# Sink columns as one float32r product for both heads, weights' first loads at other steps, and another start

## The chip, the cores and the metric

The kernel runs on one core of one Trainium2 chip. The metric is device time in microseconds (us), the median of three runs. The engines are TensorE (PE, with its weight loads as PEld), VectorE (DVE), ScalarE (ACT), GpSimd (POOL) and SyncE (SP), which issues most of the DMAs.

## What is computed

Causal attention with a window of 128 keys and 4 "sink" keys that every query sees, then two feed-forward layers. Batch 2, 8 heads, 768 positions, head size 64; the layers have 512 inputs, 2048 hidden units and 512 outputs, over 1536 tokens.

```python
scores = scale * np.matmul(q, k.transpose(0, 1, 3, 2))
is_sink = pos[None, :] < int(n_sink)
in_window = (rel >= 0) & (rel < int(window))
scores = np.where(is_sink | in_window, scores, -1000000000.0)
a = np.exp(scores - np.max(scores, axis=-1, keepdims=True))
a = a / (np.sum(a, axis=-1, keepdims=True) + 1e-09)
x = np.matmul(a, v)               # heads joined: 1536 x 512
h = x @ w_in;  g = np.where(h >= 1, h, np.where(h <= -1, 0, (h + 1) ** 2 / 4));  x = g @ w_out
h = x @ w2_in; g = h * np.clip(h + 3, 0, 6) / 6;                                 out = g @ w2_out
```

## The kernel before

The attention comes first and takes about a sixth of the time. Its work is cut into 16 pairs: a pair is two heads and up to four blocks of 128 queries (`GROUPS` gives four sorts of pairs, four of each: blocks 0 to 3 of the first batch, blocks 4 and 5, blocks 0 and 1 of the second batch, blocks 2 to 5). A block of a pair is a unit. The host has put the sink keys beside each block's window, so that a unit's scores are one product of up to 260 columns for each head (128 keys of the block before, 4 sinks, 128 keys of its own).

The code makes a list of steps and then runs it; two units are scored, then two units that were scored four units ago are turned, and when a pair is complete it is mixed:

- `load` and `load_v` issue a pair's q, k and v on SP (the first k on ACT). Three buffers of each are there, so a later load waits for an earlier pair's last use. SP works its queue in order.
- `score` (L425): two float32 products on PE; DVE adds the mask and takes the row's extreme (L448); ACT takes the exponentials and their sums (L484).
- `normalise` (L458): DVE makes the reciprocals of the sums (L459, L460); the probabilities are scaled, most of them on POOL (L475), some on ACT or DVE (L477, L479). For units with a separate sink part (w over 256) DVE writes the scaled sink columns into `psk` (L462).
- `turn` (L506): PE transposes the probabilities (L520, L521), ACT or DVE copies them out of PSUM (L502, L504).
- `sinks` (L524): PE transposes a whole pair's `psk` at once (L527), and DVE multiplies it by a mask of ones, `own`, into `pts` (L530), so that each query block keeps only its own 32 rows.
- `mix` (L536): the products with v, for each head its own half of the output partitions (L562). The last two are the sinks' share: `pts` against `vs`, in which v's four sink rows stand for each head in each 32 rows.

`vs` is filled by `load_sinks` (L404): 16 small DMAs on SP straight from v, after a memset on POOL. POOL's first work is a list in order: masks, the identity, then the memsets of `vs`, `own` and `psk` (L582 to L587).

A product with float32r operands is used for the layers: each operand is split into a rounded float32r part and the rest, and three products are added. In the attention all products are float32. PE's and SP's instructions stand in program order; the other engines' order is set by a scheduler at build time, and the names of engines for many copies by a small table of costs.

While the attention runs its last steps, the first weights are loaded in halves (`halves`, L991: the number is of steps left), narrowed from 64 to 32 bits in pieces on ACT and DVE (`narrow`, L184), and the first hidden groups (`h_group`) are put between the steps. Behind the attention the memory of its tiles is used again: `combine_x` (L754) starts with DMAs on POOL's queue (L784), and behind them on that queue stands the spill of a weight tile (L272) whose buffer the next weight waits for.

Of the kernel before, what the change touches and what calls it, by code (L numbers as in the profile page):

```python
# [8 lines left out]
F32 = mybir.dt.float32  # L9
# [7 lines left out]
P = 128  # L17
# [55 lines left out]
def sink_attention_moe_moe_kernel(  # L73
# [257 lines left out]
    NS = sink_columns(n_sink) if fast else 0  # L331
    KB = P + NS
# [13 lines left out]
    def build_fast_attention(at_p):  # L346
# [33 lines left out]
        def load(j):  # L380
# [8 lines left out]
            parts = [slice(0, P), slice(P, 2 * P), slice(2 * P, None)] if j == 0 else [slice(None)]  # L389
# [9 lines left out]
        vs = at_p.tile([P, B, DM], F32, name="vs", bufs=1)  # L399
        pts = [at_p.tile([P, NQ, P], F32, name=f"pts{n}", bufs=1) for n in range(2)]  # L400
        psk = [at_p.tile([P, NQ, SR], F32, name=f"psk{n}", bufs=1) for n in range(DIST)]
        own = at_p.tile([P, NQ], F32, name="own", bufs=1)

        def load_sinks():  # L404
            for b in range(B):
                for e in range(2):
                    for r in range(e * NS, P, SR):
# [17 lines left out]
        def score(j, u):  # L425
# [32 lines left out]
            def normalise():  # L458
                nc.vector.tensor_scalar_add(out=sm, in0=sm, scalar1=1e-9)  # L459
                nc.vector.reciprocal(out=sm, in_=sm)  # L460
                if w > 2 * P:
                    nc.vector.tensor_tensor(  # L462
                        out=psk[j % DIST][:, u - 1:u + 1, 0:2 * NS].rearrange("p u (e s) -> p u e s", e=2),
                        in0=p4[:, :, P:KB].rearrange("p (u e) s -> p u e s", e=2),
                        in1=sm.rearrange("p (u e) -> p u e", e=2).unsqueeze(3).to_broadcast([P, 2, 2, NS]), op=ALU.mult,
                    )
                end = units.index((j, u)) >= len(units) - 4
# [56 lines left out]
        def sinks(j, us, nq):  # L524

            ps = bank("ps_k")[:, 0:P]
            nc.tensor.transpose(ps, psk[j % DIST].rearrange("p u s -> p (u s)"), ident)  # L527
# [8 lines left out]
        def mix(j):  # L536
# [9 lines left out]
            for e in range(2):  # L546
                cs = slice(e * D, (e + 1) * D)
                te = t[:, e].rearrange("p n k q -> p (n k q)")
                for kb in range(nb):
# [4 lines left out]
                    ops[e].append((u0, u1 + 1, tv[:, kb, cs], te[:, c0:c1]))  # L554
                o = 0 if i0 == 0 else 1
                ops[e] = ops[e][o::2] + ops[e][1 - o::2]
                if sink:
                    ops[e].append((us, nq, ts[:, cs], tsink[:, us:nq, :].rearrange("p n q -> p (n q)")))
            for n in range(len(ops[0])):
                for e in range(2):  # L560
                    u0, u1, l, r = ops[e][n]
                    nc.tensor.matmul(  # L562
                        ps[e * D:(e + 1) * D, u0 * P:u1 * P], l, r, start=n == 0, stop=n == len(ops[0]) - 1
                    )
# [10 lines left out]
        def begin():  # L575
            load(0)
            load_v(0)
# [3 lines left out]
            with tc.manual_schedule(engines={mybir.EngineType.Pool}):  # L581
                prepare()  # L582
                make_identity(nc, ident)
                for t in (vs, own, *psk):
                    nc.gpsimd.memset(t, 0.0)
# [397 lines left out]
    with tc.manual_schedule(engines={mybir.EngineType.PE, mybir.EngineType.SP}):  # L983
# [3 lines left out]
        if fast:  # L987
            with tc.tile_pool(name="at", bufs=2) as at_p:
                build_fast_attention(at_p)
                fills = {9: (0, 0, 0), 5: (0, 0, 1), 2: (0, 1, 0)}  # L990
                halves = {56: ("i", 0), 50: ("i", 1), 44: ("o", 0), 36: ("o", 1)}  # L991
# [125 lines left out]
```

## Time and profile before

| | |
|---|---|
| median of 3 runs | 604.55 us (604.28 to 604.63) |
| the profiled execution | 603.75 us, of which 602.0 us are the span from the first to the last instruction |
| PE busy | 590.9 us, 98% |
| DVE busy | 472.3 us, 78% |
| ACT busy | 393.8 us, 65% |
| POOL busy | 109.5 us, 18% |
| chain that ended last | PE 84%, DVE 7%, ACT 4%, POOL 2% |

Busy time is what the profiler saw an engine work; PE's matmuls overlap, so that a busy PE is not a PE at its peak, and the spacing of starts says more than the length of one. The chain that ended last is followed back from the last instruction, at each step to what released it. Times in rows are from the span's start.

### The profile page before, as it was taken

To read this page: it belongs to the slowest core of one execution; us is meant where nothing else is said; L and a number is where in the kernel's file an instruction comes from. 1 tells how busy PE (TensorE), PEld (TensorE's weight loads), DVE (VectorE), ACT (ScalarE), POOL (GpSimd) and SP (SyncE) were. 2 spreads that over 40 slices of the span, in tenths; PEclk is the share of its full clock that TensorE was granted. 3 is DMA by queue.
4 is the path that set the end of the run, shared out by engine and by line. 5 is a ranking of instruction groups with operands and counts; after the bars stand their busy time and mean duration, and the time that the engine had idled before them with its cause. 6 is when DMAs were issued, how large, how long until landed. Compare 5 with 4: busy or idle time off the path is not lost.

```text
span 602.0 us, 8261 instructions
## 1 busy us (share of the span) xinstructions
PE 590.9 (98%) x2872; PEld 473.4 (79%) x2872; DVE 472.3 (78%) x865; ACT 393.8 (65%) x702; POOL 109.5 (18%) x163
## 2 busy tenths in 40 slices
PE   7999899999999999999999999999999999999997
PEld 5666567887888888888888888888888888888885
DVE  5888899799788878577799898897888875666652
ACT  6888897686566665576788785565556545454442
POOL 8676741201011101110000001111011210000000
PEclk9999999999999999999999999999999999999999
DMA  4447713966567676666457105777767555964303
GB/s 143 140 115 243 265 22 106 332 222 225 160 185 235 187 232 180 186 208 234 170 183 271 72 0 175 197 223 212 207 185 235 140 168 152 326 228 139 106 1 140
DMA packets 41786, 107.63 MB, mean 179 GB/s; under 512 B 3728, under 2 KB 13968, under 8 KB 41744
## 3 DMA queue, kind: packets, MB, share of 16 engines
q1 hardware_dynamic: 29872, 72.09, 37.5%
q0 software_dynamic: 11296, 34.61, 18.9%
q8 instruction: 23, 0.38, 0.3%
q10 hardware_dynamic: 576, 0.40, 0.2%
q14 instruction: 19, 0.16, 0.1%
HBM read 69.34 MB, written 35.65 MB: 174 GB/s over the span
## 4 chain that ended last, share of the span: by engine, by line
PE 84%; DVE 7%; ACT 4%; POOL 2%; issue 1%; DMA 1%; POOLq 0%; DVEq 0%
PE ps_y L934 42%; PE ps_h L699 35%; PE ps_v L562 3%; ACT p L484 2%; PE ps_s L435 2%; POOL p L475 1%; DMA wo_d<-w 1%; PE ps_t L521 1%; DVE p L448 1%; PE ps_t L520 1%; DVE w L224 1%; DVE x L773 1%; ACT pt L502 1%; ACT w L198 0%; DVE xt L145 0%
## 5 line engine op out<-in xcount | busy, mean ns | idle before, releaser
L934 PE MATMUL ps_y<-gh,wo 128*128 128x512 f32 x768 | 241.8, 389 | 0.0
L934 PEld LDWEIGHTS ps_y<-gh,wo 128*128 128x128 f32 x768 | 144.2, 188 | 30.0
L934 PE MATMUL ps_y<-gl,wo 128*128 128x512 f32 x384 | 149.8, 390 | 0.3 <-DVE gl L145 0.2
L699 PE MATMUL ps_h<-xh,wi 128*128 128x512 f32 x432 | 140.6, 390 | 0.0
L699 PEld LDWEIGHTS ps_h<-xh,wi 128*128 128x128 f32 x432 | 81.1, 188 | 18.4 <-issue 1.6
L934 PEld LDWEIGHTS ps_y<-gl,wo 128*128 128x128 f32 x384 | 72.1, 188 | 16.4 <-DVE gl L145 1.6
L699 PE MATMUL ps_h<-xl,wi 128*128 128x512 f32 x216 | 84.2, 390 | 0.0
L475 POOL TENSOR_SCALAR p<-p,sm 128x256 f32<-128x256 f32 (+1 forms) x68 | 58.7, 877 | 25.8 <-DVE sm L460 15.7
L699 PE MATMUL ps_h<-xt,st 128*128 128x512 f32 x252 | 61.9, 389 | 0.0
L138 ACT ACTIVATE gh<-r 128x512 fp32r<-128x512 f32 x64 | 40.1, 628 | 29.8 <-PE ps_y L934 27.7
L145 DVE TENSOR_TENSOR gl<-r,gh 128x512 fp32r<-128x512 f32 x64 | 43.8, 689 | 15.7 <-ACT gh L138 15.5
L699 PEld LDWEIGHTS ps_h<-xt,st 128*128 128x128 f32 x252 | 47.2, 188 | 10.0 <-DVE hq L827 0.2
L484 ACT ACTIVATE p<-p,nm 128x260 f32<-128x260 f32 (+2 forms) x96 | 46.3, 484 | 10.8 <-DVE nm L448 10.4
L699 PEld LDWEIGHTS ps_h<-xl,wi 128*128 128x128 f32 x216 | 40.5, 188 | 8.8 <-DVE xl L145 0.4
L448 DVE CUSTOM_DVE_ANT_0 p<-ps_s,mask 128x260 f32<-128x260 f32 (+2 forms) x96 | 35.0, 397 | 6.0 <-PE ps_s L435 5.1
L714 POOL DMA_DIRECT2D h_d<-hq x32 | 18.7, 583 | 114.2 <-ACT xt L138 43.5
L679 ACT ACTIVATE r<-hq,half 128x512 f32<-128x512 f32 x32 | 22.8, 723 | 24.7 <-DVE gl L145 18.8
L272 POOL DMA_DIRECT2D wo_d<-w x16 | 8.6, 537 | 165.3 <-DVE w L224 165.3
L827 DVE TENSOR_TENSOR hq<-ps_h,p 128x512 f32<-128x512 f32 x42 | 28.9, 688 | 10.9 <-PE ps_h L699 10.8
L435 PE MATMUL ps_s<-kraw,qraw 64*128 64x260 f32 (+2 forms) x192 | 32.9, 428 | 4.3 <-DMA kraw<-k_dram 3.2
L680 DVE SCALAR_TENSOR_TENSOR r<-r,hq 128x512 f32<-128x512 f32 x32 | 21.8, 691 | 18.6 <-ACT r L679 18.5
L138 ACT ACTIVATE wo<-w 128x1024 fp32r<-128x1024 f32 (+1 forms) x17 | 17.2, 1009 | 24.4 <-DVE w L224 24.4
(109 smaller groups left out, 949.3 us busy)
## 6 DMA issues: line engine op xcount, KB each, us to landing
h_d<-hq POOLq DMA_DIRECT2D x32, 512.0 KB, 6.1
hq<-h_d SPq DMA_DIRECT2D x32, 512.0 KB
wo_d<-w POOLq DMA_DIRECT2D x16, 512.0 KB, 7.2
raw1i<-moe_w_in_dram SPq DMA_DIRECT2D x8, 1024.0 KB
wr<-wo_d SPq DMA_DIRECT2D x16, 512.0 KB
raw1o<-moe_w_out_dram SPq DMA_DIRECT2D x8, 1024.0 KB
raw0i<-moe_w_in_dram SPq DMA_DIRECT2D x7, 1024.0 KB
raw0o<-moe_w_out_dram SPq DMA_DIRECT2D x7, 1024.0 KB
```

The source lines that it names most:

```text
L138: nc.scalar.activation(out=dst, in_=src, func=AF.Copy)
L145: nc.vector.tensor_tensor(out=dst, in0=src, in1=f32(hi), op=ALU.subtract)
L435: nc.tensor.matmul(banks[e], tq[rows, u * P:(u + 1) * P], tk[rows, c0:c0 + w], start=True, stop=True)
L448: nc.vector.tensor_tensor_reduce(out=p[:, e, :], in0=banks[e], in1=masks[min(i, 2)], scale=-SCALE, scalar=BIG, op0=ALU.add, op1=ALU.min, a ...
L475: nc.gpsimd.tensor_scalar_mul(out=px, in0=px, scalar1=r)
L484: nc.scalar.activation(out=p[:, e, :], in_=p[:, e, :], func=AF.Exp, scale=-1.0, bias=nm[:, v + e:v + e + 1], accum_out=sm[:, v + e:v + e + 1],
L679: nc.scalar.activation(out=r, in_=h, func=AF.Relu, scale=1.0 / 6.0, bias=half)
L680: nc.vector.scalar_tensor_tensor(out=g, in0=r, scalar=1.0, in1=h, op0=ALU.min, op1=ALU.mult)
L699: nc.tensor.matmul(ps, a[:, kc, :], b[kc], start=start and i == 0, stop=i == len(ops) - 1, skip_group_check=not start,)
L714: nc.gpsimd.dma_start(out=h_d[m][fc // 2][:, e:e + 2, :], in_=t)
L827: nc.vector.tensor_tensor(out=dst, in0=src, in1=p1, op=ALU.add)
L934: nc.tensor.matmul(ys[dm], a[:, cs], b, start=fc == 0 and i == 0, stop=last and i == 2)
```

## The change

Four things are changed.

1. The sinks' share of a pair is one product. `vs`, `pts` and `psk` become float32r. In each 32 rows of `psk` the 16 of a head now hold the sink columns three times: rounded, the rest, rounded again; `vs` holds against them v rounded, v rounded, and v's rest. So one product of float32r gives the sum of three, over all 128 output partitions, for both heads. It stands first in `mix`, where the two it replaces stood last.
2. `vs` is made another way: one DMA brings the sink rows of v into a free weight buffer (4 partitions, 1024 numbers in each), ACT rounds them, DVE takes the rest, six small DMAs put the parts into the first 32 rows of `vs`, and three DMAs copy these 32 rows to the others. The rounding and the DMAs are put off by six steps. For each `normalise` with sinks DVE has two small operations more (L499, L500 of the new code).
3. The weights' first half loads are issued with 64, 56, 46 and 36 steps left, before with 56, 50, 44 and 36.
4. The first pair's q and k come in two parts of 256 columns and the rest, before in three of 128, 128 and the rest; and behind the issue of these loads DVE clears a tile, and PE multiplies it by itself three times.

```diff
+    split_sinks = fast and 6 * NS <= P // max(g[3] for g in GROUPS)
...
-            parts = [slice(0, P), slice(P, 2 * P), slice(2 * P, None)] if j == 0 else [slice(None)]
+            parts = [slice(0, 2 * P), slice(2 * P, None)] if j == 0 else [slice(None)]
...
+            nc.sync.dma_start(out=flat, in_=v[:, 0:NS, :].rearrange("b s f -> s b f"))
+            def split():
+                nc.scalar.activation(out=hi.bitcast(F32R), in_=flat, func=AF.Copy)
+                nc.vector.tensor_tensor(out=lo.bitcast(F32R), in0=flat, in1=hi, op=ALU.subtract)
+                for e in range(2):
+                    for n, part in enumerate((hi, hi, lo)):
+                        r = e * SH + n * NS
+                        nc.sync.dma_start(out=heads(f32(vs[r:r + NS]), e), in_=heads(part, e))
+                for u in range(1, NQ):
+                    nc.sync.dma_start(out=f32(vs[u * SR:(u + 1) * SR]), in_=f32(vs[0:SR]))
+            defer(split, 6)
...
+                    if split_sinks:
+                        parts = t[:, :, 0:3 * NS].rearrange("p u (n s) -> p u n s", s=NS)
+                        nc.vector.tensor_copy(out=parts[:, :, 0::2, :], in_=ts.unsqueeze(2).to_broadcast([P, 4, 2, NS]))
+                        nc.vector.tensor_tensor(
+                            out=parts[:, :, 1, :], in0=ts, in1=f32(parts[:, :, 0, :]), op=ALU.subtract
+                        )
...
+            whole = sink and split_sinks
+            if whole:
+                nc.tensor.matmul(
+                    ps[:, us * P:nq * P], ts, tsink[:, us:nq, :].rearrange("p n q -> p (n q)"), start=True, stop=False
+                )
...
+            still = at_p.tile([P, P], F32, name="still", bufs=1)
+            nc.vector.memset(still, 0.0)
+            for _ in range(3):
+                nc.tensor.matmul(bank("ps_w")[:, 0:P], still, still, start=True, stop=True)
...
-                halves = {56: ("i", 0), 50: ("i", 1), 44: ("o", 0), 36: ("o", 1)}
+                halves = {64: ("i", 0), 56: ("i", 1), 46: ("o", 0), 36: ("o", 1)}
```

The queue of SP near the start, before the change (line numbers of the old code; a name on the left of `<-` is what is written):

```order
L394 DMA qraw<-q_dram 128x512
L395 DMA kraw<-k_dram 128x520
L408 DMA vs<-v_dram 4x4x64 x16
L394 DMA qraw<-q_dram 128x512
L395 DMA kraw<-k_dram 128x520
L394 DMA qraw<-q_dram 128x256
L395 DMA kraw<-k_dram 128x392
```

The same place now (line numbers of the new code, in which L395, L396 and L450 issue q, k and v):

```order
L417 DMA vsraw<-v_dram 4x2x512
L395 DMA qraw<-q_dram 128x512
L396 DMA kraw<-k_dram 128x520
L425 DMA vs<-vsraw 4x8x64 x6
L427 DMA vs<-vs 32x1024 x3
L395 DMA qraw<-q_dram 128x256
L396 DMA kraw<-k_dram 128x392
```

The fourth pair's q and k stand ahead of what fills `vs`, before behind it; the nine DMAs of `vs` depend on each other and on ACT and DVE, the sixteen did not.

ACT's exponentials of the first units, before:

```order
L484 ACTIVATE p,sm<-p,nm 128x260
L477 ACTIVATE p<-p,sm 128x256
L484 ACTIVATE p,sm<-p,nm 128x260 x3
L484 ACTIVATE p,sm<-p,nm 128x128 x2
L484 ACTIVATE p,sm<-p,nm 128x256 x2
```

and now (L520 are the exponentials, L513 the scaling; the DVE's subtraction L421 that takes L420's result stands on DVE ahead of the two masks of 128 columns):

```order
L520 ACTIVATE p,sm<-p,nm 128x260
L513 ACTIVATE p<-p,sm 128x256
L520 ACTIVATE p,sm<-p,nm 128x260
L420 ACTIVATE vsraw<-vsraw 4x1024
L520 ACTIVATE p,sm<-p,nm 128x260 x2
L520 ACTIVATE p,sm<-p,nm 128x128 x2
L520 ACTIVATE p,sm<-p,nm 128x256 x2
```

The rounding of the sink rows stands in the middle of the second two units' exponentials.

PE at the first `mix`, as a difference of the two (the numbers of lines and buffers are each side's own):

```order
L562 MATMUL ps_v<-pt,vraw 64x256 x6
L562 MATMUL ps_v<-pt,vraw 64x128 x2
L562 MATMUL ps_v<-pts_128,vs 64x256 x2
L435 MATMUL ps_s<-kraw,qraw 128x260 x4
```

and now:

```order
L599 MATMUL ps_v<-pts_128,vs 128x256
L605 MATMUL ps_v<-pt,vraw 64x256 x6
L605 MATMUL ps_v<-pt,vraw 64x128 x2
L465 MATMUL ps_s<-kraw,qraw 128x260 x4
```

The one sink product is the first of the mix, so that `vs` and `pts` have to be there before any of the mix is done.

## Rows read from the trace of the kernel before

**Rows 1.** Busy time by stage: PE, PEld, DVE, ACT, POOL, granted clock, DMA share, GB/s.

```profile
35.00:49.00 14.00, 13.77 (x118) 9.76 (x118) 11.83 (x55) 12.85 (x43) 10.33 (x13) 1.00 0.37 105
49.00:62.00 13.00, 12.18 (x107) 8.12 (x105) 10.88 (x55) 11.29 (x41) 7.48 (x11) 1.00 0.89 297
62.00:71.64 9.64, 8.69 (x65) 5.74 (x66) 8.93 (x45) 8.69 (x31) 8.13 (x9) 1.00 0.99 336
...
98.00:114.00 16.00, 16.00 (x82) 11.99 (x81) 13.13 (x18) 10.11 (x15) 4.60 (x6) 1.00 0.72 240
```

**Rows 2.** The chain that ended last, attention: start, length, what.

```profile
5.76 0.57 POOL psk L585 x4
...
35.02 1.40 PE ps_s L435 x6
```

**Rows 3.** The same chain behind the attention.

```profile
101.69 1.26 POOL x L784 x2
...
129.06 2.81 PE ps_y L934 x11
```

**Rows 4.** Timeline of PE: the first mix and one with 512 sink columns.

```profile
15.07 0.44 PE L521 MATMUL ps_t<-ident,p 128*128 128x128 f32 x2
...
16.00 1.73 PE L562 MATMUL ps_v<-pt,vraw 128*64 128x256 f32 x16
17.57 0.60 PE L562 MATMUL ps_v<-pts,vs 128*64 128x256 f32 x4
18.10 0.71 PE L435 MATMUL ps_s<-kraw,qraw 64*128 64x260 f32 x4
...
73.42 1.03 PE L562 MATMUL ps_v<-pts,vs 128*64 128x512 f32 x4
74.38 0.93 PE L435 MATMUL ps_s<-kraw,qraw 64*128 64x260 f32 x6
```

**Rows 5.** Timeline of PE: float32r products of 512 columns in a hidden group.

```profile
85.83 0.39 PE L699 MATMUL ps_h<-xl,wi 128*128 128x512 f32 x1
86.06 0.63 PE L699 MATMUL ps_h<-xh,wi 128*128 128x512 f32 x2
```

**Rows 6.** Timeline of ACT, DVE and POOL in the first 16 us.

```profile
8.22 0.50 ACT L484 ACTIVATE p<-p,nm 128x260 f32<-128x260 f32 x1
...
9.54 0.18 DVE L460 RECIPROCAL sm<-sm 128x4 f32<-128x4 f32 x1
9.82 0.17 DVE L462 TENSOR_TENSOR psk<-p,sm 128x16 f32<-128x16 f32 x1
9.92 0.35 DVE L479 TENSOR_SCALAR p<-p,sm 128x256 f32<-128x256 f32 x1
...
9.89 5.07 POOL L475 TENSOR_SCALAR p<-p,sm 128x256 f32<-128x256 f32 x6 [0.49 <-DVE sm L460]
...
13.38 0.51 ACT L484 ACTIVATE p<-p,nm 128x260 f32<-128x260 f32 x1 [1.65 <-DVE nm L448]
```

**Rows 7.** Groups of instructions: a tile of 1024 numbers a row on ACT.

```profile
L138 ACT ACTIVATE wo<-w 128x1024 fp32r<-128x1024 f32 (+1 forms) x17 | 17.2, 1009 | 24.4 <-DVE w L224 24.4
```

**Rows 8.** SP's queue at the start, and the first product that waits for a load.

```profile
0.73 1.33 SPq L394 DMA_DIRECT2D qraw<-q_dram  x3
...
2.96 1.78 PE L435 MATMUL ps_s<-kraw,qraw 64*128 64x128 f32 x8 [2.96 <-DMA kraw<-k_dram]
...
5.75 10.81 SPq L408 DMA_DIRECT2D vs<-v_dram  x16
```

**Rows 9.** Busy time in single microseconds, columns as in rows 1: when the first loads end.

```profile
8.00:9.00 1.00, 1.00 (x7) 0.65 (x4) 0.61 (x6) 1.00 (x5) 1.00 (x2) 1.00 0.68 247
9.00:10.00 1.00, 1.00 (x6) 0.70 (x5) 0.52 (x4) 1.00 (x6) 0.51 (x2) 1.00 0.02 4
```

**Rows 10.** PE's waits from 60 to 80 us: total, times, longest.

```profile
PE ps_v L562 <- DMA vraw<-v_dram: 0.8, 1, 0.8
```

**Rows 11.** Timeline of DVE at 88 us: the sinks' mask of the mix that starts at 88.75.

```profile
88.58 0.68 DVE L530 TENSOR_TENSOR pts<-ps_k,own 128x512 f32<-128x512 f32 x1
```

More of the change, by code (lines that the diff above doesn't have):

```diff
@@ L398, in build_fast_attention, with heads, load_split_sinks @@
         SR = P // NQ
-        vs = at_p.tile([P, B, DM], F32, name="vs", bufs=1)
-        pts = [at_p.tile([P, NQ, P], F32, name=f"pts{n}", bufs=1) for n in range(2)]
-        psk = [at_p.tile([P, NQ, SR], F32, name=f"psk{n}", bufs=1) for n in range(DIST)]
-        own = at_p.tile([P, NQ], F32, name="own", bufs=1)
+        SH = SR // 2
+        SD = F32R if split_sinks else F32
+        vs = at_p.tile([P, B, DM], SD, name="vs", bufs=1)
+        pts = [at_p.tile([P, NQ, P], SD, name=f"pts{n}", bufs=1) for n in range(2)]
+        psk = [at_p.tile([P, 2 * NQ, SH], SD, name=f"psk{n}", bufs=1) for n in range(DIST)]
+        own = at_p.tile([P, NQ], F32, name="own", bufs=1)
+        def heads(t, e):
+            return t.rearrange("s b (h e d) -> s b h e d", e=2, d=D)[:, :, :, e, :]
+        def load_split_sinks():
+            t = raw_p.tile([P, 2, DM, 2] if wide else [P, 2, DM], I32 if wide else F32, tag="raw", name="vsraw")
+            t = t.rearrange("p a f w -> p (a f w)") if wide else t.rearrange("p a f -> p (a f)")
+            flat, hi = (
+                t[0:NS, n * B * DM:(n + 1) * B * DM].bitcast(F32).rearrange("s (b f) -> s b f", b=B) for n in range(2)
+            )
+            lo = flat
+            nc.sync.dma_start(out=flat, in_=v[:, 0:NS, :].rearrange("b s f -> s b f"))
[9 more added lines that the diff above has]
+            defer(split, 6)
         def load_sinks():
+            if split_sinks:
+                load_split_sinks()
+                return
             for b in range(B):
                 for e in range(2):
-                    for r in range(e * NS, P, SR):
+                    for r in range(e * SH, P, SR):
                         nc.sync.dma_start(
@@ L526, in sinks @@
             ps = bank("ps_k")[:, 0:P]
-            nc.tensor.transpose(ps, psk[j % DIST].rearrange("p u s -> p (u s)"), ident)
+            nc.tensor.transpose(ps, f32(psk[j % DIST].rearrange("p u s -> p (u s)")), ident)
             shape = [P, nq - us, P]
@@ L554, in mix @@
                     ops[e].append((u0, u1 + 1, tv[:, kb, cs], te[:, c0:c1]))
+                if split_sinks:
+                    continue
                 o = 0 if i0 == 0 else 1
@@ L562, in mix @@
                     nc.tensor.matmul(
-                        ps[e * D:(e + 1) * D, u0 * P:u1 * P], l, r, start=n == 0, stop=n == len(ops[0]) - 1
+                        ps[e * D:(e + 1) * D, u0 * P:u1 * P], l, r, start=n == 0 and not whole,
+                        stop=n == len(ops[0]) - 1,
                     )
@@ L584, in begin @@
                 for t in (vs, own, *psk):
-                    nc.gpsimd.memset(t, 0.0)
+                    nc.gpsimd.memset(t.bitcast(F32), 0.0)
                 for u in range(NQ):
```

8 lines of the change are left out of this document (5 added, 3 removed).

## Prediction

> **What bounds the kernel now.** I read the stages first, then the chain that ended last, then the timelines at the places of the change. From 98 us on PE works without a gap: 16.00 of 16.00 us, and the granted clock is 1.00 [rows 1]. Nothing of the change lies behind the attention. The chain there runs from the end of the attention (POOL's DMAs at 101.69, which wait for the attention's memory) over a spilled tile, ACT and DVE to PE at 129.06, 27.4 us later [rows 3], and PE works through the same 27 us without a gap. So both move with the end of the attention, and I count only what moves that end.
>
> Within the attention the chain has three parts. Until 35 us it goes from POOL's memsets (the last ends at 6.33) over DVE and ACT, and PE stands in it only at the first mix. At 35.02 PE takes it over [rows 2]. From 35 to 62 us PE is busy 13.77 of 14.00 and 12.18 of 13.00 us, but ACT too has only 1.15 and 1.71 us left, and from 62 to 71.64 DVE has 0.71 of 9.64 us left [rows 1]. Whatever PE saves there is soon asked of ACT and DVE.
>
> **What the sinks' product saves on PE.** Two float32 products of 256 columns take 0.53 us from their start to that of the scores behind them (17.57 to 18.10), of 512 columns 0.96 us (73.42 to 74.38) [rows 4]. One float32r product of 512 columns takes 0.23 us from start to start (85.83 to 86.06) [rows 5]; one of 256 no less than half, 0.12, and no more than 0.23. Some 0.1 us of the old times is the handing over to another kind of product, which stays. So a mix with 256 columns saves 0.53 - 0.1 - 0.12 = 0.3 us (0.2 to 0.4), one with 512 columns 0.96 - 0.1 - 0.23 = 0.63 (0.6 to 0.73). There are eight of the first and four of the second. Three of the first (17.57 us and the next two) lie where PE is not on the path, and give nothing. The other five give 5 x 0.3 = 1.5 us; since ACT has 2.9 us left in 27, I take 1.0 (0.3 to 1.5). The four with 512 columns give 2.5. From it comes off the mix at 88.75: its sinks stand first now, and its mask is ready only at 88.58 + 0.68 = 89.26 us [rows 11], 0.5 us too late. Another 0.3 I take off for DVE (next part). That leaves 1.7 (1.0 to 2.4).
>
> **What it adds on DVE.** Two more small operations for each of 16 normalisations with sinks. The old one, L462, takes 0.17 us; what does not depend on it starts 0.10 behind it, and it started 0.28 behind the reciprocal that it needed (9.54, 9.82, 9.92) [rows 6]. So a pair costs 0.2 us if other work stands between, 0.4 if not: 3.2 to 6.4 us in all, of which DVE hides most in waits. On the path I count two of them before 35 us, 0.3 us in all, beside the 0.3 above.
> The Trainium skill ("VectorE: DVE Perf Modes", section on the TRN2 errata) says that many small tiles pay a fixed cost in each instruction, 58 cycles; that speaks against splitting one small operation into three. By its figure the 32 operations would cost an estimated 2.5 us (75 to 95 ns each), less than the rows give, and the 0.6 us on the path would be 0.3.
>
> **What filling vs costs.** Before, sixteen independent DMAs held SP for 10.81 us, and mix one did not wait for them [rows 8, 4]. Now ACT needs the loaded rows in the middle of its exponentials, at 8.22 us [rows 6]. SP issues that load at about 5.0 us, behind 2 MB of q, k and v; those are through at about 8.7 us (DMA share 0.68 in the ninth microsecond, 0.02 in the tenth) [rows 9]. So ACT waits until 8.8 and then works 1.0 us on 1024 numbers a row [rows 7], until 9.8; DVE's subtraction of the same size, which stands ahead of two maskings, ends at 11.0 (I price it like ACT's). The four operations behind it, some 1.1 us, put the reciprocal's end at 12.1, so that POOL's six scalings start at 12.15 and not at 9.89, and end 5.07 us later at 17.2 [rows 6]. PE's transposes wait for them (15.07 before) and the mix follows 0.93 behind, at 18.2, where it started at 16.00 [rows 4].
> The other way to the mix is the DMAs. Sixteen took 10.81 us, 0.68 each; the first two go at 9.85, the third waits for DVE until 11.0, the sixth is issued at 13.0 to 13.7. From issue to a product that uses the load the first k took 2.23 us (0.73 to 2.96) [rows 8]. So the copies start at 15.2 to 15.9, the last of three is issued by 17.2 at a third of 1.33 us each [rows 8], and vs is whole at 18.4 to 19.4. I take 18.5 for the mix, and the scores behind it, 0.3 us shorter, 2.2 us later than 18.10. DVE's own shift at the maskings is 1.4 to 2.2, so 2.0 of it stay. With 0.3 for the small operations the start costs 2.3 us (0.8 to 4.0: from a load that is there when ACT comes, to rounds of DMAs a third slower).
> The Trainium skill ("DMA: Bandwidth & Descriptors", section Anatomy of one DMA) gives about 2.0 us fixed and the bytes over 436 GB/s. Its fixed part agrees with the 2.23 us. By it alone, with no queue ahead, the rows would be there at an estimated 7.0 us, ACT would not wait, and the start would cost 0.6 us less: the first rival.
>
> **The other edits.** The weights' halves are only issued earlier. PE's one wait for a load, 0.8 us for v at 62 us [rows 10], should go, since a half ahead of that v then stands where the DMAs were less busy (35 to 49 us: share 0.37, then 0.89) [rows 1]. ACT is late there too, so I take 0.3 (0 to 0.8). The two parts of q and k and the three products of zeros I cost at nothing: PE's first product waits for k until 2.96 anyway, and three products of 128 columns with a DVE memset fit before (the first eight matmuls, 768 columns, took 1.78 us) [rows 8]. A larger first part makes the first scores later by the transfer of 128 KB, up to 0.5 us, under the cover of POOL's memsets, which hold DVE until 6.33 [rows 2]. The granted clock reads 1.00 throughout, so it does not tell whether PE starts at its level of 1.2 GHz; if the zeros brought 2.4 GHz earlier, the first scores would save up to half of 1.78 us, also under that cover and that of the load for vs. Without cover these edits are worth -0.9 to +0.5.
>
> **The sum.** Back come 1.0 + 1.7 + 0.3 = 3.0 us (1.3 to 4.7); the start costs 2.3. That is -0.7 against the profiled execution, 603.75 to 603.05; the median of the runs lies 0.8 above it, so 603.8 us. This kernel can tell about 0.2%, 1.2 us, from no change.
>
> **Rivals.**
> - *The start hides it.* ACT did not work without a gap there: it waited 1.65 us for DVE before its exponentials at 13.38 [rows 6]. If the sink rows land by 8.2 and POOL's chain catches up, the start costs 0.6, and with ACT keeping pace 3.9 comes back: 603.75 - 3.3 + 0.8 = 601.3. For it: the load is only 16 KB and small loads can pass. Against it: one queue, and 2 MB ahead.
> - *The mix waits for vs (the other side).* Three rounds of DMA in a row stand behind ACT and DVE. If the small ones take a third more to land, 3 us, and each of six 0.8 to issue, the copies start at 17.8 and vs is there at 22 us: PE, and behind it every score, starts 6 us late, of which 5 stay. With 3.0 back, 603.75 + 2.0 + 0.8 = 606.6. It decides from a first sink product at about 20.5 us on. For it: SP works in order and the copies wait for all six. Against it: 2.23 us for the first k.
> - *The sinks' gain is not PE's to have.* ACT and DVE, with 1.2 to 0.7 us left in a stage, set the pace from 35 to 71 us, and POOL's scalings the rest: back come 1.0, and the start costs 2.3: 605.8.
>
> **How the numbers follow.** The sum with its bounds has 0.42 (602.2 to 605.2 by itself), the hidden start 0.32, the wait for vs 0.14, no gain 0.12. Faster by over 0.2% (below 603.3): a third of the first case and nearly all of the second, 0.43. Slower (above 605.8): the third, half of the fourth and a little of the first, 0.23. Within: 0.34. The range reaches to both rivals' middles, 600.8 to 606.6.
>
> **What would show it.** The first sink product starts at 18 to 19 us, with a wait on DMA or on POOL ahead; ACT's operation on 1024 numbers lies at 8.8 us behind a short wait for its load; the sink product is one of 0.12 to 0.23 us; PE's wait for v at 62 us is gone; the attention's last mix ends about 0.7 us earlier than 100.9; from there all rows are shifted by that. If the last mix is earlier by 3 us, the start was hidden or the zeros and parts did more than nothing; if it is later, look for PE's wait at the first mix, then for DVE full from 35 to 98 us. The forecast is also wrong if the time from the last mix to the end changes by over 1 us.

## The result and the profile after

The changed kernel takes 612.08 us (median of five runs, 609.58 to 614.62) against 604.55 (603.91 to 604.92): a ratio of 1.0128, with an interval of 1.0111 to 1.0146. It is slower by 7.5 us; the forecast was 603.8, and 612 lies outside its range. The runs after also lie 5.0 us apart, those before 1.0.

The profiled run is the slowest of the five, 614.62 us. Against the profiled 603.75 of before its 10.9 us more come in three places. The end of the attention's last mix is at 107.24 us and not at 100.98: 6.3 us. From there to the last long stretch of `ps_y` products (514.81, before 508.05) it takes 0.5 us more. And that stretch, 89.82 us without a gap before, takes 93.89.

The start first: PE's timeline, start and length in us, with what ended an idle time in brackets.

```profile
13.02 2.31 PE L465 MATMUL ps_s<-kraw,qraw 64*128 64x260 f32 x8 [1.72 <-DVE nm L478]
...
21.29 0.55 PE L599 MATMUL ps_v<-pts,vs 128*128 128x256 f32 x1 [0.17 <-issue]
21.78 3.25 PE L605 MATMUL ps_v<-pt,vraw 128*64 128x256 f32 x16
24.96 1.40 PE L465 MATMUL ps_s<-kraw,qraw 64*128 64x260 f32 x6
```

The scores behind the first mix start at 24.96 us, in [rows 4] at 18.10: 6.9 us, where I forecast 2.2. The first mix itself takes 3.25 us for sixteen products, in [rows 4] 1.73: PE's transposes stand 0.21 us apart until 20.7 us, at the lower of its two levels (1.2 GHz), and 0.11 apart only behind this mix; before, they were 0.11 apart from 12 us on. The granted clock of these windows reads 1.00 in both, so here only the spacing tells.

What holds the start shows on the other engines and on SP (SPq) in the same microseconds.

```profile
4.65 0.38 SPq L417 DMA_DIRECT2D vsraw<-v_dram  x1
7.66 0.36 SPq L395 DMA_DIRECT2D qraw<-q_dram  x1
8.06 0.43 SPq L396 DMA_DIRECT2D kraw<-k_dram  x1
10.45 1.06 ACT L420 ACTIVATE vsraw<-vsraw 4x1024 fp32r<-4x1024 f32 x1 [1.81 <-DMA vsraw<-v_dram]
11.54 1.21 DVE L421 TENSOR_TENSOR vsraw<-vsraw 4x1024 fp32r<-4x1024 f32 x1 [2.98 <-ACT vsraw L420]
11.57 4.29 SPq L425 DMA_DIRECT2D vs<-vsraw  x6
13.84 4.93 POOL L511 TENSOR_SCALAR p<-p,sm 128x256 f32<-128x256 f32 x6 [4.00 <-DVE sm L490]
17.31 1.86 SPq L427 DMA_DIRECT2D vs<-vs  x3
```

The 16 KB for `vs` are issued at 4.65 us and are there when ACT starts at 10.45. ACT stands still for them 1.81 us, DVE behind ACT 2.98, POOL behind DVE 4.00, and its scalings start at 13.84 instead of 9.89 [rows 6]. The three copies into `vs` are issued by 19.17 us, and the first sink product follows 2.1 us later.

The chain that ended last goes to this product over POOL and PE:

```profile
13.84 2.85 POOL p L511 x3
...
16.73 0.48 PE ps_t L556
...
18.06 1.58 PE ps_s L465 x8
...
21.12 0.17 issue
21.29 0.55 PE ps_v L599
```

From 16.73 to 21.12 PE works at its lower level, and it stands idle for only 0.17 us before the product. In e4 and e8 (below), where PE did wait for the copies, the product also stands 2.1 us behind their issue. So two ways end here within 0.2 us of each other: the one over POOL and a slow PE, and the one over the DMAs into `vs`.

The end, in the chain that ended last, and PE's waits from 100 us on (total, times, longest).

```profile
514.81 2.73 PE ps_y L982 x12
...
520.12 8.57 DMA hq<-h_d
...
530.87 77.83 PE ps_y L982 x335
```

```profile
PE ps_y L982 <- ACT gh L138: 1.6, 1, 1.6
PE ps_y L982 <- DVE gl L145: 0.9, 2, 0.6
PE ps_h L747 <- DVE xl L145: 0.7, 1, 0.7
```

A transfer of `hq` back from `h_d` (512 KB) takes 8.57 us; ACT and DVE wait for it, and PE for them. Behind that wait the granted clock falls for a while:

```profile
530.00:540.00 10.00, 9.63 (x34) 7.59 (x35) 7.73 (x12) 5.70 (x10) 0.00 (x0) 0.83 0.88 344
```

By this mean some 3.4 us passed at half speed, an estimated 1.7 of the 4.1 us that the stretch lost. Before, PE waited 0.2 us in the whole time behind 100 us. No line of the diff works in this stage.

### The profile page after: what moved, and what is told of

Same layout as the page of the kernel before. It is cut to its first block, busy times and chain, and to the rows that moved or that the text cites. A ratio compares the mean times of both kernels' runs of the same rounds, so it can differ in the third digit from the quotient of the medians.

```text
span 612.8 us, 8239 instructions
## 1 busy us (share of the span) xinstructions
PE 596.8 (97%) x2842; PEld 477.8 (78%) x2842; DVE 478.6 (78%) x899; ACT 395.1 (64%) x703; POOL 108.6 (18%) x163
## 4 chain that ended last, share of the span: by engine, by line
PE 82%; DVE 5%; DMA 4%; ACT 3%; POOL 3%; issue 1%; SPq 0%; POOLq 0%; ACTq 0%; DVEq 0%
PE ps_y L982 40%; PE ps_h L747 36%; POOL p L511 2%; PE ps_v L605 2%; PE ps_s L465 2%; ACT p L520 2%; DMA hq<-h_d 1%; DMA wo_d<-w 1%; PE ps_t L557 1%; DMA vsraw<-v_dram 1%; DVE p L478 1%; PE ps_t L556 1%; DVE xl L145 1%; DMA kraw<-k_dram 0%; DVE w L224 0%
## 5 line engine op out<-in xcount | busy, mean ns | idle before, releaser
L520 ACT ACTIVATE p<-p,nm 128x260 f32<-128x260 f32 (+2 forms) x96 | 46.4, 484 | 12.2 <-DVE nm L478 11.3
L465 PE MATMUL ps_s<-kraw,qraw 64*128 64x260 f32 (+2 forms) x192 | 34.4, 447 | 3.2 <-DVE nm L478 1.7
L879 POOL DMA_DIRECT2D h_d<-ct x14 | 16.0, 1142 | 84.4 <-DMA h_d<-hq 57.1
```

What stands on the lines that cost most here:

```text
L465: nc.tensor.matmul(banks[e], tq[rows, u * P:(u + 1) * P], tk[rows, c0:c0 + w], start=True, stop=True)
L520: nc.scalar.activation(out=p[:, e, :], in_=p[:, e, :], func=AF.Exp, scale=-1.0, bias=nm[:, v + e:v + e + 1], accum_out=sm[:, v + e:v + e + 1],
```

## The experiments

Fourteen kernels. "MM" is the number of matmuls on the profile page (2872 before, 2842 after; each has one weight load beside it). The fetch (start of the packet of PE's code nearest to the last stretch), the last stretch of `ps_y` products and its length are explained with the third group. Instruction counts in the expectations (5838 before, 5784 changed) are of PE's whole program. e3, e5, e6 and e11 leave out some or all of the sinks' share of the result. Times in us, places from the profiled run of each.

| run | median | before beside it | ratio (interval) | first mix | last mix ends | MM | fetch | last stretch | its length |
|---|---|---|---|---|---|---|---|---|---|
| before | 604.55 | | | 16.0 | 101.0 | 2872 | 505 | 508.1 | 89.8 |
| after | 612.08 | 604.55 | 1.0128 (1.0111 to 1.0146) | 21.3 | 107.2 | 2842 | 520 | 514.8 | 93.9 |
| e1_split_only | 609.42 | 604.09 | 1.0089 (1.0066 to 1.0112) | 21.1 | 104.9 | 2836 | 519 | 513.0 | 91.2 |
| e2_rest_only | 604.33 | 604.09 | 0.9999 (0.9990 to 1.0009) | 16.4 | 101.3 | 2878 | 505 | 508.7 | 89.8 |
| e3_no_fill | 607.99 | 604.09 | 1.0065 (1.0048 to 1.0081) | 17.0 | 100.6 | 2842 | 514 | 508.4 | 92.8 |
| e4_early_load | 609.73 | 604.09 | 1.0101 (1.0072 to 1.0130) | 19.3 | 103.0 | 2842 | 516 | 510.7 | 92.0 |
| e5_pad | 609.75 | 604.18 | 1.0088 (1.0073 to 1.0103) | 23.4 | 107.3 | 2878 | 510 | 514.1 | 89.8 |
| e6_fewer_pe | 604.90 | 604.18 | 1.0013 (1.0002 to 1.0023) | 16.4 | 99.8 | 2836 | 516 | 508.7 | 90.0 |
| e7_mended | 608.01 | 604.18 | 1.0060 (1.0045 to 1.0075) | 21.8 | 105.7 | 2872 | 509 | 512.3 | 89.8 |
| e8_no_zeros | 609.95 | 604.18 | 1.0096 (1.0077 to 1.0116) | 20.4 | 104.1 | 2836 | 518 | 512.1 | 90.2 |
| e9_small_pad | 607.28 | 604.04 | 1.0053 (1.0040 to 1.0065) | 20.6 | 104.3 | 2872 | 508 | 511.0 | 89.8 |
| e10_best | 604.58 | 604.04 | 1.0008 (0.9999 to 1.0017) | 18.2 | 102.1 | 2872 | 505 | 508.7 | 89.8 |
| e11_fewer7 | 608.17 | 604.04 | 1.0066 (1.0053 to 1.0080) | 16.2 | 100.0 | 2844 | 514 | 509.1 | 92.6 |
| e12_late_new | 607.31 | 604.35 | 1.0052 (1.0039 to 1.0066) | 20.7 | 106.1 | 2872 | 510 | 512.7 | 89.8 |
| e13_late_fill | 603.71 | 603.96 | 0.9999 (0.9990 to 1.0008) | 17.2 | 101.5 | 2872 | 505 | 508.0 | 89.8 |
| e14_no_pad | 606.75 | 603.96 | 1.0044 (1.0031 to 1.0057) | 17.2 | 101.6 | 2848 | 514 | 510.0 | 91.0 |

**Which part of the change.** e1_split_only takes the zeros out and puts the parts and the halves back.

```diff
-            parts = [slice(0, 2 * P), slice(2 * P, None)] if j == 0 else [slice(None)]
+            parts = [slice(0, P), slice(P, 2 * P), slice(2 * P, None)] if j == 0 else [slice(None)]
-            for _ in range(3):
-                nc.tensor.matmul(bank("ps_w")[:, 0:P], still, still, start=True, stop=True)
-                halves = {64: ("i", 0), 56: ("i", 1), 46: ("o", 0), 36: ("o", 1)}
+                halves = {56: ("i", 0), 50: ("i", 1), 44: ("o", 0), 36: ("o", 1)}
```

> The changed kernel without the zeros, with q and k of the first pair in the old three parts and the weights' halves at their old steps: the sinks' product and the new filling of vs alone. Theory A (the filling of vs holds the start by some 7 us and nothing takes it back): 609 to 612.5 us, the first sink product at 20 us or later. Rival B (the zeros, the parts or the halves did it, with the sinks' product harmless): 603 to 605.5 us, first sink product before 19 us. Rival C (the start is caught up and DVE's two small operations for each normalisation cost the time, from 35 us on): 609 to 612 too, but the first sink product at 20 us and the shift of the rows growing behind it.

e2_rest_only is the opposite: `split_sinks = False`.

> The changed kernel with the sinks as before (two float32 products for a mix, sixteen DMAs into vs): the zeros, the two parts and the new steps of the halves alone. Theory A: 603.3 to 605.8 us, no change that can be told, first mix at 15.5 to 16.8 us. Rival B: 607 us or more. Rival C: as theory A.

e1 lost 5.3 us, e2 nothing: rival B falls, the sinks' part does it.

**What the filling of `vs` does.** e3_no_fill drops it, e4_early_load issues its load on ACT's queue behind the first k.

```diff
             if split_sinks:
-                load_split_sinks()
                 return
```

> The changed kernel, but vs is only cleared and never filled, so that the sinks' share of v is left out: no load of the sink rows, no rounding, no subtraction, none of the nine DMAs; the product of the sinks, the small operations on DVE, the zeros, the parts and the halves stay. Theory A: the start is back at 16 to 17 us for the first mix and the time is 601 to 605 us; if the product saves what I forecast for it (2.7 us) it is 602. Rival C: 608 us or more. Rival B: 608 us or more.

```diff
-            nc.sync.dma_start(out=flat, in_=v[:, 0:NS, :].rearrange("b s f -> s b f"))
+            nc.scalar.dma_start(out=flat, in_=v[:, 0:NS, :].rearrange("b s f -> s b f"))
```

> The changed kernel with the load of the sink rows issued on ACT's queue behind the first pair's k, ahead of all other pairs' loads; the rounding on ACT then comes ahead of the exponentials, and SP's nine DMAs of vs are issued where they were. Theory A, and the load's queue is the heart of it: the rounding lies before 6 us, ACT and DVE lose nothing, the nine DMAs go from about 8.5 us on, the first sink product starts at 15.5 to 17.5 us, and the time is 603 to 607 us. Theory A, but the nine DMAs are the heart of it: first sink product still at 18.5 us or later, 607 to 610 us. Rivals B and C: 610 to 613 us.

Without the filling the attention is back: first mix at 17.0 us, and its last mix ends 0.4 us earlier than before (100.59). Theory A is right as far as 101 us, and rival C falls, since DVE's small operations are still there. But the time was 608, not 602: in the profiled run 3.6 us more than before lie behind the attention, 0.7 of them ahead of the last stretch. There the chain that ended last reads:

```profile
508.35 2.73 PE ps_y L981 x12
...
513.82 8.84 DMA hq<-h_d
...
524.85 76.26 PE ps_y L981 x335
```

From 508.35 to 601.11 it takes 92.76 us, 2.9 more than the 89.82 of before. None of my theories had that. e4 moved the first sink product to 19.29, where PE still waited 1.59 us for the DMAs, and lost 2.1 in the same late place. So with the rows there early the first mix still comes 2.3 us later than without the filling (19.29 against 16.96), 1.6 of it PE's wait for these DMAs.

**The late stall.** SP, ACT, DVE and PE run the same instructions there as before, in the same order and, up to this transfer, at the same distances. What stands elsewhere is one packet of a queue that the DMA view calls "instruction" (q8). It comes about every 29 us in this stage. 396 products take 89.82 us, so 128 of them, with their weight loads 256 instructions, take 29.0: it is PE's code, 16 KB of it at a time. In the kernel before it comes at 505 us, when the DMA engines rest (queue, kind: packets, MB, share; from 505 to 506 us).

```profile
q8 instruction: 1, 0.02, 6.3%
```

In the changed one it comes at 520 (from 519.5 to 521.5 us), together with the transfers of `hq`:

```profile
q1 hardware_dynamic: 335, 0.64, 97.1%
q8 instruction: 1, 0.02, 2.8%
q14 instruction: 1, 0.01, 1.0%
```

Each sinks' product saves PE three matmuls and three weight loads; in twelve mixes that is 72 instructions, less 12 for the zeros. So the fetch, counted in instructions, comes 60 later, some 7 us, and meets `hq`. That was theory D. The packet of 8 KB on q14 is not the cause: e11 (below) stalls with none of its kind between 496 and 543 us, and e9, with one at 515.8, 4.8 us behind the stretch's start, does not stall. e5_pad and e6_fewer_pe test theory D from both sides.

```diff
+            pad = bank("ps_w")[:, 0:8]
+            for _ in range(18):
+                nc.tensor.matmul(pad, still, still[:, 0:8], start=True, stop=True)
```

> The kernel of the run without the filling of vs (the sinks' share of v is left out here too), with 18 tiny float32 products of zeros more at the start, on PE's idle time before the first k. They give PE 72 instructions (36 products, 36 weight loads) back, as many as the one sinks' product saves over the old form in twelve mixes. Theory D (the late stall, PE waiting 2 to 3 us at 521 to 525 us for hq from h_d, comes from PE's own code: its fetch of 16 KB, which comes every 30 us, has moved by 72 instructions, some 8 us, into the transfer of hq): the fetch near the end lies at 504 to 507 us again, the transfer of hq takes 4 to 6 us and not 8 to 9, PE does not wait there, and the time is 603 to 605.5 us against 608.0 without the pad. Rival E (the stall comes from the sinks' DVE work, from the buffers' places or from an attention that ends at another time): 607 us or more, the stall still there.

```diff
-                if sink:
+                if sink and j % 4 == 3:
                     ops[e].append((us, nq, ts[:, cs], tsink[:, us:nq, :].rearrange("p n q -> p (n q)")))
```

> The kernel before, with the two float32 products of the sinks left out in nine of the twelve mixes that have them (so the sinks' share is missing in these): PE has 72 instructions fewer, everything else, the filling of vs, DVE's work and the DMAs are those of before. Theory D: the late fetch of PE's code moves to 511 to 515 us, the stall for hq is there though nothing of the change is, and the time is 605 to 608 us although PE has 6 us less to do in the attention. Rival E: no stall, and 602.5 to 604.5 us. By either, the products taken away also measure what PE can gain in the attention: by the rival of my prediction, the end of the attention (POOL's DMAs at 101.69 before) comes 0.3 to 1.2 us earlier; by my main sum 3 us.

e5's stall is gone: the last stretch is 89.8 us without a gap, and its runs lie 0.3 us apart. But its time was missed, because the pad itself was not hidden:

```profile
2.52 7.69 PE L626 MATMUL ps_w<-still 128*128 128x8 f32 x36
```

36 products of 8 columns take 0.21 us each, as much as a transpose of 128 columns at that level of the clock; so here the weights' side sets it, not the columns. The start was 6.5 us later for it. e6 was half a miss: the fetch moved to 516, 6.8 us behind the last stretch's start, and the profiled run shows no stall there; ten runs spread from 603.75 to 606.16. It also measured something else: with 6.1 us less of products on PE (six pairs of 0.53 and three of 0.96, [rows 4]) the time from the first mix to the end of the last fell only from 84.98 to 83.44.

e9_small_pad gives the complete changed kernel the missing instructions cheaply, e11_fewer7 takes from the kernel before nearly as many as the change did.

```diff
-            for _ in range(3):
-                nc.tensor.matmul(bank("ps_w")[:, 0:P], still, still, start=True, stop=True)
+            pad = bank("ps_w")[0:32, 0:8]
+            for _ in range(18):
+                nc.tensor.matmul(pad, still[0:32, 0:32], still[0:32, 0:8], start=True, stop=True)
```

> The changed kernel, complete, with 18 float32 products of 32 rows and 32 columns by 8 in place of the three large products of zeros: PE has as many instructions as before (within 3) instead of 54 fewer. The large pad of the earlier run made the start 6.5 us later (its 36 products took 7.7 us); these have a quarter of the weights' columns and I expect 1.9 to 4 us for them, so that the first scores still wait for k or begin up to 1 us later. Theory D: the fetch near the end is back at 510 to 512 us, 3 us ahead of the transfers of hq instead of 5 us behind the start of the last stretch, PE does not wait for hq, the runs agree within 0.6 us instead of 5, and the time is what the start alone costs: 608.5 to 611. Rival E: the stall and the spread are as in the changed kernel, 611 to 613.5.

```diff
-                if sink:
+                if sink and j > 6:
```

> The kernel before with the sinks' two products left out in the first seven mixes (their share is missing there): PE has 58 instructions fewer than before, 4 fewer than the changed kernel; with nine mixes left out it had 75 fewer, its late fetch came 6.8 us behind the start of the last stretch and the time spread from 603.8 to 606.2. Theory D: the fetch now comes 5 to 5.6 us behind the start of the last stretch, as in the changed kernel, PE waits there 1 to 3 us for hq, and the time is 605 to 607.5 us with a spread of over 1 us, though PE has 3.7 us less to do. Rival E: 603 to 604.5 us, no late wait.

e9 took 4.8 us off the changed kernel, more than forecast, by adding instructions: 607.28, with runs 0.9 us apart. Between the profiled runs it is 7.8 us, 5.0 of them behind the attention and 2.9 ahead of its end, where e9 runs its first mix at the upper level of the clock. e11 made the kernel before 4.1 us slower by taking 3.7 us of work away. Its attention ends 1.0 us earlier, then 2.1 us are lost ahead of the last stretch, and then comes (chain, and PE's waits from 500 to 540 us):

```profile
509.12 2.73 PE ps_y L934 x12
...
514.57 8.74 DMA hq<-h_d
...
525.50 76.26 PE ps_y L934 x335
```

```profile
PE ps_y L934 <- ACT gh L138: 2.0, 1, 2.0
```

This is the changed kernel's stall in a kernel that has none of its parts. Rival E falls.

The DMA view shows one thing more in the stalled runs. POOL issues a transfer of its own into `h_d` (`h_d<-ct`, queue q0) 5.1 us behind the start of the last stretch, before and after alike. From 8.0 to 9.5 us behind that start the changed kernel has

```profile
q1 hardware_dynamic: 61, 0.21, 52.2%
q0 software_dynamic: 14, 0.03, 35.3%
```

and the kernel before

```profile
q1 hardware_dynamic: 111, 0.40, 83.5%
```

So POOL's transfer runs beside that of `hq`, on whose queue (q1) half as much is moved. The same overlap is in e3, e4 and e11, the other runs whose last stretch is over 2 us longer, and in none of the rest.

**The clock at the start.** e8_no_zeros is the changed kernel without the three products of zeros.

> The changed kernel without the three products of zeros. In the profiled run of the changed kernel the first mix takes 3.25 us, near 1.2 GHz by the spacing of its products, without the zeros, parts and halves (the run of the split alone) 1.73 us. If the zeros, followed by PE's longer wait, are what keeps the clock low until 26 us: first mix 1.7 to 1.9 us long, second mix at 27 to 28 us against 29.8, and 608.5 to 610.5 us. If it is the parts, the halves or chance: as the changed kernel, 611 to 613 us.

It came to 609.95, and its first mix takes 1.73 us, not 3.25. The zeros alone are not the reason, since e2, e3 and e4 have them and run the first mix at full rate. A long wait of PE alone is not either: e9 (small pad) waited 2.91 us for DVE ahead of 12.26, still at the lower level by the spacing of its transposes, and ran the first mix at full rate. e12_late_new (below) waited as long ahead of 17.71, and its first mix was slow again. There the granted clock shows it (0.50, columns as in [rows 1]); it fell while PE waited, from 14.88 to 17.71:

```profile
17.71 1.57 PE L477 MATMUL ps_s<-kraw,qraw 64*128 64x256 f32 x4 [2.83 <-DVE nm L490]
...
20.68 3.04 PE L613 MATMUL ps_v<-pt,vraw 128*64 128x256 f32 x16
```

```profile
16.54:23.36 6.82, 5.64 (x24) 3.53 (x26) 4.91 (x22) 4.83 (x18) 3.71 (x5) 0.50 0.07 12
```

Whether the zeros and a wait together kept the clock low in the changed kernel stays open.

**Versions that mend it.** e7_mended and e10_best load the sink rows early, put in the whole filling at once, and let the sinks' product stand last in the mix; e7 has the large pad, e10 the small one.

```diff
-            defer(split, 6)
+            fill.append(split)
...
-                load_split_sinks()
+                fill.pop()()
```

> The changed kernel with four mendings: the sink rows are loaded on ACT's queue behind the first k; the rounding, the subtraction and the nine DMAs are put in at once and not six steps later, so that the DMAs stand ahead of the fourth pair's loads; the sinks' product is the last of the mix; and 18 tiny products of zeros take the place of the three large ones, so that PE has as many instructions as before. If the filling (theory A) and PE's code fetch (theory D) are the two causes: first sink product at 16.5 to 18.5 us, no late stall, 603 to 605.5 us. If DVE's small operations cost more than I see (rival C): 606 to 608 us. If the early filling takes ACT, DVE or the queue from the first scores: first mix later than 18 us, 606 to 609 us.

> The mended kernel (sink rows loaded on ACT's queue, all of the filling put in at once, the sinks' product last in the mix) with the small pad instead of the large one. Theories A and D together: first mix at 16 to 17.5 us, attention's last mix ends at 100 to 101.3 us (98.8 to 100.1 if the 1 us that the mixes gained in the runs without the filling stays), no late stall, 602.8 to 604.8 us. If the early filling still holds the start (rounding and subtraction ahead of the first scores on ACT and DVE): first mix later than 18 us, 605 to 607.

e7 fell to its pad, like e5 (first mix at 21.8). e10 reached 604.58: no stall, but a first mix at 18.2 us. e12_late_new leaves the first four pairs their old products, and puts off the filling of `vs` for the others.

```diff
+        def split_pair(j):
+            return split_sinks and j >= 4
...
+                defer(load_split_sinks, 8)
...
-            whole = sink and split_sinks
+            whole = sink and split_pair(j)
```

> A version made from what the runs showed, complete: the first four pairs, of which three lie where PE is not on the path, keep the old two float32 products and their eight small DMAs; the other eight mixes with sinks use the one float32r product, last in the mix, and their vs is filled behind the first mixes; q and k in three parts and the halves as before; 12 tiny products of zeros at the start bring PE's instructions to 5842 (5838 before, 5784 changed). Theories A and D: first mix at 16 to 17 us, no late stall, the attention ends 0.5 to 1.3 us earlier than before (100.98 for its last mix), 602.3 to 603.7 us. If the rounding and subtraction of 1024 numbers on ACT and DVE cost the same wherever they stand: 603.8 to 605 us. If the single buffer of the first pairs' masks makes the mixes wait: 605 us or more.

It was a miss, 607.31: the load now stood behind the fourth pair's on SP, and DVE's subtraction, which the scheduler had put among the first maskings, waited for it. e13_late_fill moves that load to ACT's queue as e4 did; e14_no_pad is e13 without its 12 tiny products.

```diff
-            nc.sync.dma_start(out=flat, in_=v[:, 0:NS, :].rearrange("b s f -> s b f"))
+            nc.scalar.dma_start(out=flat, in_=v[:, 0:NS, :].rearrange("b s f -> s b f"))
```

> The version of the last run with one thing changed: the load of the sink rows for vs is issued on ACT's queue behind the first pair's k, so that rounding and subtraction never wait for it. By order ACT rounds between its first exponentials and DVE subtracts behind its first four maskings, where DVE waited 0.69 us for POOL before; the nine DMAs of vs stand behind the fifth pair's q and k. If the place of the load is the start's whole cost: first mix at 16 to 17 us, the attention's last mix ends at 99.7 to 101, no late stall, 602.5 to 603.9 us. If the 2.3 us of work on ACT and DVE cost what they last wherever they stand: first mix at 17.5 to 18.5 us, 604.3 to 605.5 us.

```diff
-            pad = bank("ps_w")[0:32, 0:8]
-            for _ in range(12):
-                nc.tensor.matmul(pad, still[0:32, 0:32], still[0:32, 0:8], start=True, stop=True)
```

> The same kernel without the 12 tiny products of zeros: PE has 49 instructions fewer, 5793 against 5842 (5838 in the kernel before, 5784 in the changed one). Theory D: the late fetch of PE's code comes 3 to 4.5 us behind the start of the last stretch and not 3 us ahead of it, PE waits there for hq, the time is 1 to 5 us longer than that of the padded one, and the runs spread by over 1 us. Rival E (the stall belongs to something else that the pads also change): the two within 0.8 us of each other.

e13 took 603.71 us, as long as the kernel before. e14 took 606.75: 3.0 us more, for 24 matmuls (and the clearing of their tile) less. Up to the end of the attention the two agree within 0.1 us (the last mix ends at 101.48 and 101.55). Then e13 has

```profile
508.03 89.77 PE ps_y L997 x396
```

and e14

```profile
509.96 2.73 PE ps_y L992 x12
...
515.77 5.32 DMA hq<-h_d
...
524.74 76.24 PE ps_y L992 x335
```

so 1.9 us lie between the attention and the last stretch and 1.3 in it (524.74 + 76.24 - 509.96 = 91.02). The first 1.9 have the same sign: e14's fetch comes at 110 us, into the transfers that follow the attention, e13's at 100; PE waits 1.5 us for `gl` at 130 us in e14 and not in e13.

## Why the prediction was wrong

**The end of the attention moves all behind it: half wrong.** "Nothing of the change lies behind the attention" is the step that failed outright: the sum has no term for it. The order is the same there, but PE has 60 instructions fewer ahead of it, and its code comes at another time. In the profile after, 4.6 of the 10.9 us lie there (0.5 and 4.1, the fallen clock among them); in e14 against e13, which differ in the tiny products alone, 3.1. I had read the order of the engines, not the DMA rows of their code. The test that I named ("the forecast is also wrong if the time from the last mix to the end changes by over 1 us") caught it. The Trainium skill ("Runtime: NRT & Kernel Launch", section Instruction fetch mechanics) says that code is refilled in blocks of 16 KiB, 256 instructions, and that this is mostly hidden. The size agrees with the one packet of 0.02 MB every 29 us; that it is hidden does not hold here, though it is not PE that waits for code.

**What filling `vs` costs: 2.3 us forecast, 6.3 to 7 measured.** The mechanism was right to each link (load, ACT, DVE, POOL, DMAs), the sizes were not. First, I let the load through at 8.7 us, when the DMA share of [rows 9] falls to nothing. But a pair's q and k that the sixteen DMAs had kept back until 16.7 us before now went out at 7.66 and 8.06, and the DMAs stayed busy: the share in the ninth to eleventh microsecond is

```profile
8.00:9.00 1.00, 0.89 (x6) 0.92 (x8) 0.55 (x4) 0.64 (x3) 1.00 (x3) 1.00 0.73 193
9.00:10.00 1.00, 1.00 (x5) 0.35 (x4) 0.00 (x0) 0.00 (x0) 0.85 (x1) 1.00 0.87 294
10.00:11.00 1.00, 1.00 (x6) 0.89 (x5) 0.00 (x0) 0.55 (x1) 0.00 (x0) 1.00 0.53 204
```

where 0.02 stood for the tenth before. I had shown that very move of the order in the change's section and had not counted its half megabyte. That these loads, issued behind the rows, held the rows up is argued; no run has the new load with the old order. The miss is 1.7 us at ACT (10.45 against 8.8), and the same at POOL (13.84 against 12.15). With it the rival "The start hides it" fell. (The prediction's estimate of 7.0 us took from the Trainium skill, "DMA: Bandwidth & Descriptors", section Anatomy of one DMA, what is fitted there for DMAs that POOL issues; this load is on SP's queue.) Second, the DMA rounds: I priced the copies' issue as done at 17.2, it was 19.17, 0.3 us more than came with the rows; and from there to the first sink product I had 1.3 us, it took 2.1 (21.29 against 18.5). Third, the lower clock of the first mix, 1.5 us (3.25 against 1.73), was not in the sum at all. The rival "the mix waits for vs" had nearly the size (6 us, 5 to stay) but only one of the two ways that ended together at 21.29.

**The sinks' product: 2.7 us forecast, 0.7 to 1.4 measured.** From the sinks' product to the next of the mix it takes 0.29 us with 256 columns (36.58 to 36.87) and 0.41 with 512 (78.13 to 78.54), where I had 0.22 and 0.33 with the handing over; so a product saves 0.24 and 0.55, nearly what I said. But PE is not what sets the pace. From first mix to last: 84.98 us before, 83.63 in e3, 83.71 in e9, 84.31 in e13 (which has the new product in eight of twelve mixes). And e6, with 6.1 us taken off PE, gained 1.5. The rival "the sinks' gain is not PE's to have" (1.0) was right on this term. A stage shows it, the same work as 35 to 49 us in [rows 1], shifted by 7 us:

```profile
41.97:55.97 14.00, 13.26 (x111) 9.24 (x111) 12.92 (x62) 12.77 (x44) 11.39 (x14) 1.00 0.47 140
```

PE's busy time falls from 13.77 to 13.26 us, DVE's rises from 11.83 to 12.92.

**DVE's small operations: priced too low.** In these rows they take 0.17 to 0.18 us each, as the old one in [rows 6]:

```profile
19.86 0.18 DVE L499 CAST psk<-pss 128x32 fp32r<-128x32 f32 x1
20.16 0.17 DVE L500 TENSOR_TENSOR psk<-pss,psk 128x16 fp32r<-128x16 f32 x1
```

But over all sixteen (busy us, mean ns) the two new ones, L499 and L500, are longer, while L494, the old one, is not:

```profile
L500 DVE TENSOR_TENSOR psk<-pss,psk 128x16 fp32r<-128x16 f32 x16 | 4.3, 270 | 0.3
L499 DVE CAST psk<-pss 128x32 fp32r<-128x32 f32 x16 | 3.5, 219 | 0.3 <-DVE nm L478 0.2
L494 DVE TENSOR_TENSOR pss<-p,sm 128x16 f32<-128x16 f32 x16 | 2.8, 172 | 0.2
```

That is 7.8 us by their lengths, where I had 3.2 to 6.4 for all; single ones last up to 0.43 us, and what stretches them is not shown. The 75 to 95 ns for one that the prediction took from the Trainium skill ("VectorE: DVE Perf Modes", section on the TRN2 errata) are less than half. The same section says that its 58 cycles are too low and that the fixed term measured is about 150 cycles; by its (N+151)/0.96 for a float32 `tensor_tensor`, 16 numbers take an estimated 174 ns. The trace agrees with that for L494 (172) and not for L500 (270). How much of the product's missing gain is theirs was not tried by itself.

**The other edits: right by themselves** (e2: 604.33 against 604.09), and the wait for v at 62 us is gone. Beside the filling, the kernel without the zeros took 2.1 us less (e8); but leaving them out moves PE's code by 12 instructions as well, and the runs of the changed kernel lie 5 us apart, so what the zeros themselves cost is not shown.

What stays open is how one 16 KB packet, by its share 2.8% of 2 us on 16 engines or 0.9 us of one, makes a transfer of `hq` three us longer. That the two meet is shown, and that moving PE's code parts them, and that the longest stalls go with POOL's transfer running beside `hq`. How the packet brings POOL's transfer forward is not shown. With the packet 5.1 to 5.4 us behind the stretch's start the stretch is 2.1 to 4.1 us longer (after, e3, e4, e11), at 4.0, 5.8 and 6.2 us 1.2, 0.4 and 1.4 (e14, e8, e1), at 6.8 us 0.1 (e6); I can't say why. The 5 us spread of the changed kernel's runs may go with it: e5, e7, e9 and e10, with the code moved back, spread by 0.1 to 0.9 us, but e12 by 1.7, and one of e13's eleven runs took 606.1. The clock may have a part too: the fastest of the five runs after (609.58) is the one with a granted clock of 1.000, the others have 0.992 to 0.997.

## What to carry to other kernels

An edit that changes how many instructions an engine has ahead of a tight place moves its code fetches there: look in the DMA view for the instruction queue's packets beside transfers that something waits for, and try a dozen tiny products before believing a loss or a gain of half a per cent. A small load put behind a full queue costs what stands in the queue and, as far as this case goes, what a removed wait lets go out beside it; price it by what is issued now, not by the queue of before. Before counting PE's savings, take the work out altogether and time that: here 6 us of PE were worth 1.5.

## What the hardware showed that I had not expected

- Twelve tiny products of zeros at the start made a complete kernel 3.0 us faster (606.75 to 603.71), 1.9 us of it between 101 and 510 us and 1.3 behind that.
- A product of 8 columns with 128x128 float32 weights took 0.21 us in the first microseconds (7.69 for 36), with 32x32 weights 0.06 (1.45 for 24):

```profile
1.08 1.45 PE L638 MATMUL ps_w<-still 32*32 32x8 f32 x24 [1.08 <-DVE still L635]
```

- PE at its lower level for the first 25 us of the changed kernel, by the spacing of its products, and again behind its wait for `hq`: a granted clock of 0.83 over ten microseconds is an estimated 3.4 us at half.
